# A fused attention and max-out feed-forward kernel whose whole order of work is replaced by another

## The chip, the cores and the metric

The kernel runs on one core of a Trainium2 chip. What is timed is the device time of one execution, in microseconds (us). The kernel before took 177.53 us in the median of three runs (176.96 to 178.75). TensorE does the matrix products and transposes (in a trace PE, with PEld for the loading of its weights), VectorE is DVE, ScalarE is ACT, GpSimd is POOL, and SyncE (SP) does nothing but issue DMAs from its queue.

## The reference

Four sequences of 768 tokens have eight heads of 64 features. Three of the heads (`is_retrieval`) see every earlier token, the other five see the first four tokens and the last 64. The attention's output, 3072 rows of 512, goes through a feed-forward layer that takes the larger of two products:

```
scores = scale * (q @ k.T)
mask   = full causal for retrieval heads, causal & (first 4 or last 64) for the others
a      = softmax(where(mask, scores, -1e9))
x      = (a @ v), heads side by side          # 3072 x 512
h1     = x @ w1                               # 512 x 1024
h2     = x @ w2
out    = maximum(h1, h2) @ w_out              # 1024 x 512
```

## The kernel before, in words

**Tiling.** A sequence is worked in two halves of 384 queries, so there are eight halves in all, (0,0), (1,0), (0,1), (1,1) and then both halves of sequences 2 and 3. Heads are taken in four pairs, and which heads form a pair is read from `is_retrieval` at run time. For each half the kernel loads q, k and v as f32 (`load_half`), casts them to bf16 (tiles `qb`, `vb`; lines 654 to 671), turns q and k (on PE at L680, copied back from PSUM into `qk`; later halves by DMA at L703), multiplies them into scores (L959), takes the exponential on ACT (L978, tile `at`), masks it on DVE (L997), multiplies it with v (L1022) and divides by the row sums (L1039 and L1049, tile `x`). The half's `x` is turned (L1148 or L1167, tile `xt`) and goes into the feed-forward product.

**The feed-forward product.** With max(h1, h2) = h2 + relu(h1 - h2) the kernel needs one wide product instead of two. `prep_weights` makes w12 = w1 - w2 in four column quarters (L1184, DVE alone), casts w2 to bf16 in four quarters (`w2b`, line 1191), turns these on PE (L1201, copied into `w2t`), and multiplies them with the cast output weights (`wob`, line 574) into w2o = w2 @ w_out (L1228, sixteen steps of two matmuls). From then on a half costs the "up" product with w12 (L1251, 8 blocks of 4 matmuls), the relu (L1276 on ACT, L1278 on DVE) and the "down" product, x times w2o plus the relu's output times wob (L1308). The casts and copies all go through one helper (`copy`, L382 on ACT, L384 on DVE and POOL), so in a profile they are told apart by their tiles. The very first half takes v in another way: eight casts of its rows into a spare `xt` tile, then three PE products with a shifted identity (L723) that put the rows in place, then three copies into `vb`.

**The loads at the start.** SP issues in order q, k and v of half (0,0), the two halves of w2 (1 MB each), three quarters of w_out (0.5 MB each), a half of w1, the last quarter of w_out and the other half of w1. All go through the same queue.

**What sets the order.** Nothing decides it when the kernel is built. Each step is an `Op`, registered in a fixed order and numbered. `Order.run` (line 154) walks the string `PLAN` and emits op after op: a token such as `127v` says that op 127 comes next and goes to DVE (`p` PE, `a` ACT, `v` DVE, `g` POOL, `s` SP), the digits behind a `p` name the PSUM banks, and `x0*40` says forty idle matmuls into bank 0 (`dummy`). Each engine works off its own share of that list in order, and waits at each instruction until its inputs are there; an instruction that waits holds up everything behind it on its engine. The table thus fixes three things at once: the order on each engine, which engine does a cast or copy that several could do, and which PSUM banks are used.

Of the kernel before, what the change touches and what calls it, by code (L numbers as in the profile page):

```python
# [173 lines left out]
65a x3*2 52g x3*5 8s 31a 55v x3 61g x3*2 56p3 33a 53v x4*3 4s 63a x4*2 69g x4 50p4 71a 57v x5 66p5 51a 58p6  # L174
28g x7 74p7 67a 59v x0*2 26g 76p01 75a 25g 79p23 9s 34a 37v 78a 36v 6s 35v 39a 82p45 77a 41g 85p67 84a 40a
88p10 83a 86a 13s 119v 91p54 38a 123v 89a 11s 46p6 87a 93a 42p1 47v 92a 44p7 80a 43v 16s 124p4 81a 127v 120p6
45a 131v 128p5 125a 104p2 121v 106p 94p1 90a 96p 107v 5v 95p3 10g 100p 132p7 109v 105p4 97v 101v 110p 108v
135p6 98v 149p0 111v 99v 7a 136p2 113v 134p1 103v 14s 138p 112v 133v 139p 150p 129v 137p 15s 122v 142p 151p
141p 12g 102v 140p 118v 116p4 114p7 143p 117v 115a 152p 145p 153a 147p 18s 130v 146a 212p5 144a 208p3 126v
213a 148a 221p4 209v 210p7 19s 154a 178g 192a 194g 166v 219p0 211a 156v 164v 198p6 180v 160p1 170p5 199a 220v  # L180
217p2 171a 222v 184p3 21s 165a 167g 223p7 161v 155a 157g 218a 185v 181g 172p6 162p0 195g 179a 206p5 224v 173a
193g 17s 163a 174v 186p4 200p1 176v 187a 207v 237p23 241p76 420s 201v x0 239a 244p04 214p5 190v 242a 204v 188v
245a 202v 238a 225p 247v 243a 240v 246a 249p13 20s 253p70 251a 257p26 248v 216p4 250a 252v 254a 423s 169v 168g
183a 227p 197a 196g 255a 175g 205v 177a 234p 182a 158a 256v 258a 261p31 228p 191v 259a 189v 421s 203v 263a
260v 159a 275p7 262a 270p0 235a 265p2 264v 271p 266p 229a 276p6 236s 272v 267v 281p 274v 277p 215p1 268v 24s
306a 289g 290v 305a 316g 226p 273v 295a 269v 315g 296a 424s 278v 309p3 282v 279v 231p 310a 284v 283v 23s 293p4
280v 319p5 311v 294a 313v 287p0 232v 285p2 320a 299p3 288v 356p67 286v 360p41 357a 363p05 422s 300v 339p2 358a
365a 323v 329p6 359v 22s 450g 442a 441v 337p7 364a 230s 427v 361a 333p3 434v 547s 321v 340a 433v 325p5 362a
301v 334v 449a 327p0 303v 326a 438v 454g 330v 428a 331p4 338a 328v 446a 335p2 233s 431g 448v 426a 440g 366p13
332a 447v 369p56 374p70 367a 432g 551s 307v 318a 341p4 376a 425g 668s 336v 368a 451p1 375a 439g 308v 342p 298a  # L190
291g 371a 452v 312g 343p 370a 317g 373v 800s 377p03 297g 324a 381p27 453v 385p61 378a 314g 351p5 302v 382a
292g 322a 372v 435p0 549s 383a 393p2 436v 394p 344a 304g 429p7 387a 395p 548s 384v 400p4 386a 396p 401p 437v
430a 389p01 397v 388v 406p6 669s 391a 352p 399v 398v 390a 407p7 379a 392v 353p 380v 408p 402p 354a 675s 553v
568g 412p 346p1 409v 403v 569a 413v 411v 559g 558a 405v 347p 552g 670s 579a 414v 578a 410v 556p2 404v 348p
415v 672s 557a 418p0 349a 562p3 419v 671s 416p5 563a 486p64 417v 490p72 350s 488a 493p10 443p3 495a 455p5 444v
802s 491a 457p4 494a 456v 487a 469p0 673s 458v 492a 465p7 445v 489v 470a 496p31 550s 466a 499p56 504p42 498a
507p07 500a 463p1 564v 508a 566v 502v 509a 467p5 464v 804s 501a 459p0 510v 506a 468v 461p7 503v 497a 676s 678g
460v 700a 523p1 505a 692g 462v 524p 525p 699g 691v 683a 806s 526p 511p65 561a 570g 515p23 555a 581v 519p07
345s 512a 684g 481p4 527v 696s 560v 521a 516a 571g 529v 476p6 528v 517a 580v 520a 530p7 677v 531p 518v 695s
513a 532p 582p2 522v 565a 572p1 583a 537p3 514v 682s 477p 573a 533v 586v 534v 542p 536p0 535v 688s 587g 538p  # L200
478p 543v 576v 577a 575g 539v 544v 482p 540v 807s 541v 585g 554a 545v 483p 479v 574v 546s 619p52 567v 484a
584v 623p17 626p03 697v 471p6 624a 628a 689v 704s 625a 630v 472p 627a 620a 629v 473p 355s 621a 674s 622v
631p41 652p3 633a 474v 635p70 632a 639p52 634v 636a 643p14 647p6 640a 653p 648p 803s 598p7 654v 649v 641a 656v
609p5 655v 644a 480s 645a 705v 651v 637a 590p2 650v 703s 599a 642v 588p1 591a 638v 596p3 681s 685a 680g 694v
686a 702g 679a 658p4 646v 589a 657p0 594p6 693a 475s 701a 698v 690a 659p 706v 592p7 597a 660v 595v 687s 663p
600p2 662v 593a 664v 661v 602p1 601a 799s 665v 666v 614p3 603a 926s 738p67 742p02 739a 745p41 610p 485s 743a
801s 744a 611p 746a 740a 615p 612a 741v 616p 747a 924s 748p60 617v 751p24 667s 749a 756p75 752a 759p13 775p6
761a 776p 754v 604p2 757a 762v 750a 805s 809v 825g 605p 824a 814v 835a 815g 613s 758a 606p 828s 808g 760a 753a
777p 778p 763p37 607a 755v 767p05 779v 834a 771p14 781v 782p2 819s 765a 780v 783p 768a 784p 711p7 785v 769a
787v 838s 817g 709p6 786v 811a 816g 836a 770v 821g 713p0 823a 772a 812s 837v 715p5 764a 826a 714v 707p2 841a  # L210
810g 818s 822v 820v 717p1 716a 843v 766v 708a 719p3 710a 718v 813s 773a 789p0 827v 721p5 712v 720a 831v 833a
723p2 774v 608s 839s 722v 788p6 790p 794p 733p1 791v 795v 792v 829s 796v 724p 797v 793v 725p 928s 875p47 726a
879p35 882p06 734p 881a 883a 925s 842v 840v 884a 885v 735p 876a 798s 832v 886v 877a 830v 728p2 736v 880a 878v
887p50 891p64 889a 895p73 932s 903p1 892a 890v 904p 908p0 896a 905v 729p 907v 893a 927s 906v 888a 730p 894v
897a 727s 898v 909p 899p67 913p4 901a 731v 914p1 900a 929s 854p5 910v 902v 912v 865p3 911v 930s 855v 915p 919p
848p7 916v 920v 917v 844p6 922v 931s 849a 921v 858p2 918v 845a 732s 850p0 859a 856p5 923s 955a 934v 956g 933a
852p7 940g 857v 947a 948a 846p1 938s 853a 870p4 851a 847v 939a 949g 935v 937s 871p 936a 942a 957v 958a 950v
941v 872p 954a 962v 946g 866p 873v 944s 867p 973p6 868a 943s 994p25 974v 998p70 995a 1001p14 952s 975p3 945v
996a 1003a 977p6 997v 951s 1000a 976v 965p2 1002a 971p5 999a 966v 978a 967p4 960s 972v 1004p03 968v 969p1
1006a 959s 953v 1005a 1007p72 970v 1012p65 1009a 1015p43 737s 1019p01 1008a 1011v 1031p2 874s 1017a 1032p  # L220
1010v 1033p 618s 1014a 1018v 1034p 961v 984p7 869s 1013a 1035v 1036v 1016a 1037v 1038p3 1020a 1039p 1040p
1021a 1023p56 1041v 1027p42 1042v 1025a 963p0 1022v 1029a 860p1 1043v 1028a 964v 1024a 1044p6 1030v 985p 1026v
1046p 986p 1047v 1048v 1049v 1045p2 1050p 989p3 1051v 1052v 1053v 990p 1054s 1091v 991p 1092p4 979p0 992a
1093v 993s 980p 981p 861p 982a 983s 862p 1061p5 863a 1067p6 864s 1062a 1071p2 1068a 1055p3 1081p0 1056v 1059p1
1057p5 1060v 1063p6 1058v 987a 1069p4 1064v 988s 1065p3 1070a 1076p1 1066a 1072p 1077p 1078p 1073p
"""

LAST = """
1079v 1082p 1080s 1074a 1083p 1075s 1086p5 1084v 1087p 1088p 1085s 1089a 1090a
"""  # L230


# [89 lines left out]
def tile_three_full_heads(  # L322
# [3 lines left out]
    nc = tc.nc  # L326
# [34 lines left out]
    banks = [psum.tile([128, 512], F32, name=f"ps{e}") for e in range(8)]  # L361
# [220 lines left out]
    for what in LOADS:  # L582
        kind, c = what[:2], int(what[2:]) if what[:1] == "w" else 0
# [1188 lines left out]
```

## Time and profile before

| what | value |
|---|---|
| median of three runs | 177.53 us |
| the profiled execution's own time | 178.13 us |
| its span, first to last instruction | 175.6 us |
| PE busy | 167.5 us (95%) |
| DVE busy | 117.6 us (67%) |
| ACT busy | 123.8 us (71%) |
| POOL busy | 35.4 us (20%) |
| moved by DMA | 36.14 MB, mean 206 GB/s |
| granted PE clock | 1.00 throughout |

Busy shares are means over stages that differ. Times inside the execution are counted from the first instruction; 2.53 us of the execution's time lie outside the span. A matmul's end is modelled: it is shown some 0.2 us after the next one has begun, so the start of one to the start of the next is the better measure. In the timeline a row stands for a run of like instructions, and "[0.70 <-DVE w2b L384]" means that the engine had been idle for 0.70 us until that instruction.

### The profile page before, as it was taken

To read this page: it belongs to the slowest core of one execution; us is meant where nothing else is said; L and a number is where in the kernel's file an instruction comes from. 1 tells how busy PE (TensorE), PEld (TensorE's weight loads), DVE (VectorE), ACT (ScalarE), POOL (GpSimd) and SP (SyncE) were. 2 spreads that over 40 slices of the span, in tenths; PEclk is the share of its full clock that TensorE was granted. 3 is DMA by queue.
4 is the path that set the end of the run, shared out by engine and by line. 5 is a ranking of instruction groups with operands and counts; after the bars stand their busy time and mean duration, and the time that the engine had idled before them with its cause. 6 is when DMAs were issued, how large, how long until landed. Compare 5 with 4: busy or idle time off the path is not lost.

```text
span 175.6 us, 4870 instructions
## 1 busy us (share of the span) xinstructions
PE 167.5 (95%) x1755; PEld 102.1 (58%) x1775; DVE 117.6 (67%) x327; ACT 123.8 (71%) x278; POOL 35.4 (20%) x80
## 2 busy tenths in 40 slices
PE   7899898999999999999999999999999999999993
PEld 7755644654675575667556546664665457545542
DVE  5546997876999587778978525895895377820511
ACT  3499416899899997999589789965749479214310
POOL 6850213411304803043301004200021000000000
PEclk9999999999999999999999999999999999999999
DMA  5999999999899999997299699245997236053104
GB/s 127 333 373 385 387 381 330 196 317 301 192 197 333 253 257 212 238 227 177 65 188 232 162 258 219 59 123 134 241 248 183 50 88 243 2 151 119 65 6 179
DMA packets 77661, 36.14 MB, mean 206 GB/s; under 512 B 59202, under 2 KB 72514, under 8 KB 77634
## 3 DMA queue, kind: packets, MB, share of 16 engines
q1 hardware_dynamic: 77488, 35.73, 76.7%
q8 instruction: 15, 0.25, 0.7%
q14 instruction: 12, 0.10, 0.2%
q10 hardware_dynamic: 146, 0.07, 0.1%
HBM read 25.17 MB, written 6.29 MB: 179 GB/s over the span
## 4 chain that ended last, share of the span: by engine, by line
PE 68%; DMA 11%; ACT 6%; issue 5%; POOL 4%; SPq 3%; DVE 2%; DVEq 0%; ACTq 0%; POOLq 0%
PE ps L1308 30%; PE ps L1251 21%; PE ps L959 7%; PE ps L1022 7%; DMA ld<-in_moe_w_out_dram 6%; DMA ld<-in_v_dram 4%; ACT at L978 4%; PE ps L680 2%; SPq L455 2%; POOL wob L384 2%; PE ps L1228 1%; POOL tab L612 1%; ACT ot L382 1%; ACT vb L382 1%; DMA raw<-in_is_retrieval_dram 1%
## 5 line engine op out<-in xcount | busy, mean ns | idle before, releaser
L978 ACT ACTIVATE at<-ps 128x512 bf16<-128x512 f32 (+2 forms) x134 | 64.8, 578 | 4.6 <-PE ps L959 4.1
L1251 PE MATMUL ps<-xt,w 128*128 128x384 bf16 x256 | 45.2, 326 | 0.1
L1308 PE MATMUL ps<-wob,g 128*128 128x512 bf16 (+2 forms) x192 | 43.8, 371 | 0.7 <-issue 0.3
L997 DVE TENSOR_TENSOR at<-at,tab 128x1024 bf16<-128x1024 bf16 (+5 forms) x49 | 25.1, 524 | 12.3 <-ACT at L978 11.4
L1251 PEld LDWEIGHTS <-w 128*128 128x128 bf16 x256 | 24.0, 98 | 15.9 <-issue 0.6
L1308 PEld LDWEIGHTS <-g 128*128 128x128 bf16 x200 | 18.3, 98 | 19.6 <-issue 0.2
L1278 DVE TENSOR_SCALAR g<-ps 128x384 bf16<-128x384 f32 x34 | 18.5, 553 | 13.5 <-PE ps L1251 13.0
L382 ACT COPY ot<-ps 128x512 f32<-128x512 f32 (+1 forms) x16 | 9.0, 571 | 22.5 <-PE ps L1308 19.1
L1308 PE MATMUL ps<-w2o,xt 128*128 128x512 bf16 (+2 forms) x90 | 24.0, 370 | 0.5
L384 POOL CAST qb<-ld 128x384 bf16 (+1 forms) x31 | 13.6, 472 | 53.3 <-DMA ld<-in_k_dram 28.4
L1049 DVE TENSOR_TENSOR x<-ps,rez 128x192 f32 x64 | 22.7, 354 | 2.0 <-DVE rez L1039 0.5
L1022 PEld LDWEIGHTS <-at 128*128 128x128 bf16 x477 | 17.9, 97 | 4.7 <-DVE at L997 0.3
L1022 PE MATMUL ps<-vb,at 128*128 128x65 bf16 x387 | 19.3, 194 | 0.0
L1276 ACT ACTIVATE g<-ps 128x384 bf16<-128x384 f32 x30 | 14.5, 495 | 6.6 <-PE ps L1251 6.4
L959 PE MATMUL ps<-qk 64*128 64x128 bf16 (+1 forms) x330 | 19.1, 229 | 0.0
L959 PEld LDWEIGHTS <-qk 64*128 64x128 bf16 x330 | 12.1, 94 | 9.2 <-issue 7.0
L382 ACT CAST qb<-ld 128x384 bf16 (+1 forms) x32 | 12.8, 458 | 2.1 <-DMA ld<-in_q_dram 1.7
L1308 PEld LDWEIGHTS <-xt 128*128 128x128 bf16 x100 | 8.8, 98 | 8.1
L382 ACT COPY qk<-ps 128x384 bf16<-128x384 bf16 (+1 forms) x17 | 10.2, 631 | 2.3 <-PE ps L680 1.9
L384 DVE COPY ot<-ps 128x512 f32<-128x512 f32 (+1 forms) x9 | 6.0, 672 | 7.3 <-PE ps L1308 6.4
L680 PE MATMUL ps<-tab,qb 128*128 128x128 bf16 x120 | 10.0, 219 | 0.7 <-POOL qb L384 0.4
L384 POOL CAST vb<-ld 128x192 bf16 x15 | 6.1, 421 | 20.3 <-issue 10.2
(76 smaller groups left out, 162.7 us busy)
## 6 DMA issues: line engine op xcount, KB each, us to landing
ld<-in_v_dram SPq DMA_DIRECT2D x21, 256.0 KB, 5.4
ld<-in_moe_w_dram SPq DMA_DIRECT2D x4, 1024.0 KB, 12.2
out_dram<-ot SPq DMA_DIRECT2D x16, 256.0 KB, 3.6
ld<-in_q_dram SPq DMA_DIRECT2D x5, 768.0 KB, 8.1
ld<-in_k_dram SPq DMA_DIRECT2D x5, 768.0 KB, 6.9
ld<-in_q_dram SPq DMA_DIRECT2D x9, 256.0 KB, 4.5
ld<-in_k_dram SPq DMA_DIRECT2D x9, 256.0 KB, 4.4
ld<-in_moe_w_out_dram SPq DMA_DIRECT2D x4, 512.0 KB, 11.0
```

Of the source, the lines that this page charges most:

```text
L382: nc.scalar.copy(out=out, in_=in_)
L384: eng[e].tensor_copy(out=out, in_=in_)
L680: nc.tensor.transpose(to[:, i], qbs[:, T["qb", n, hf] % NQB, t, i].rearrange("p h d -> p (h d)"), ident)
L959: nc.tensor.matmul(to.rearrange("p (i c) -> p i c", c=128), lhsT=lhsT, rhs=q_of(n, i, m)[rows], start=bk not in under, stop=True, skip_gro ...
L978: nc.scalar.activation(out=at[:, bk, 0:w], in_=bank(("ps", b, hf, t), part=bk)[:, 0:w], func=ACT.Exp, scale=scale,)
L997: eng[e].tensor_tensor(out=at, in0=at, in1=tbl, op=ALU.mult)
L1022: nc.tensor.matmul(po[:, hh, i - NT * hf, :], lhsT=ats[:, T["at", b, hf, t] % NAT, bk, e * 128:(e + 1) * 128], rhs=rhs, start=first, stop= ...
L1049: nc.vector.tensor_tensor(out=xs[:, HALVES.index((b, hf)) % NX, :, bass.ds(heads[2 * p + hh], 1), :], in0=po[:, hh, :, 0:D].unsqueeze(2), ...
L1251: nc.tensor.matmul(bank(key)[:, 0:HALF], lhsT=w[:, kc, fc * 128:(fc + 1) * 128], rhs=xts[:, HALVES.index((b, hf)) % NXT, :, kc, :], start= ...
L1276: nc.scalar.activation(out=g, in_=ph, func=ACT.Relu)
L1278: nc.vector.tensor_scalar_max(out=g, in0=ph, scalar1=0.0)
L1308: nc.tensor.matmul(bank(key)[:, cols], lhsT=lhsT, rhs=(w2o if kind == "x" else wob)[:, c, cols], start=(e == 0), stop=(e == len(steps) - 1),)
```

## The change

`PLAN` is another list. It has the same 1081 ops, so the same loads, casts, products and stores, in another order and with other PSUM banks; 147 of them, casts and copies above all, go to another engine than before. The idle matmuls go from 81 to 75. `dummy` gets a second parameter that would make one idle matmul several times as wide; every call leaves it at 1, so that an idle matmul is what it was. Lines move by one to four.

```
-0s x0*3 1s x0*5 2s x0*40 3s 30a 32v 68g x0*3 70a 54v x0 48p0 62a 27g x1 72p1 49v x2*4 29g 60a 73v x2 64p2 x3*2
+0s x0*3 1s x0*5 3s x0*36 2s 52a 30v x0*3 68a 54v x0 70g x0 32a x0 56p0 62a 26v 25g x1 48p1 57a 72p2 x3 49v
...
-    def dummy(e):
-        nc.tensor.matmul(banks[e][:, 0:128], lhsT=warm, rhs=warm, start=True, stop=True)
+    def dummy(e, m=1):
+        nc.tensor.matmul(
+            banks[e][:, 0:128 * m].rearrange("p (m c) -> p m c", m=m), lhsT=warm,
+            rhs=warm.unsqueeze(1).to_broadcast([128, m, 128]), start=True, stop=True,
+        )
```

**First place: the loads on SP at the start.** Before:

```order
L442 DMA ld<-in_q_dram 128x8x192
L442 DMA ld<-in_k_dram 128x8x192
L442 DMA ld<-in_v_dram 128x8x192
L547 DMA ld<-in_moe_w_dram 128x4x512 x2
L568 DMA ld<-in_moe_w_out_dram 128x2x512 x3
```

And now:

```order
L446 DMA ld<-in_q_dram 128x8x192
L446 DMA ld<-in_k_dram 128x8x192
L551 DMA ld<-in_moe_w_dram 128x4x512
L446 DMA ld<-in_v_dram 128x8x192
L551 DMA ld<-in_moe_w_dram 128x4x512
L572 DMA ld<-in_moe_w_out_dram 128x2x512 x3
```

The first half of w2 goes ahead of v. The second half of w2 keeps its place, and so does everything behind it up to the order of the three w_out quarters among themselves and of the two w1 halves (columns 512 to 1023 of w1 now come first).

**Second place: DVE where w12 is made.** `w_144` is the quarter of w1 - w2, `x` the divided output of the first half, `xt` its turned copy, `g` a relu, `w2o` the copy of a finished column block of w2 @ w_out. Before:

```order
L384 COPY w2t<-ps_167 128x1024
L384 COPY w2t<-ps_165 128x1024
L1184 TENSOR_TENSOR w_144<-ld 128x4x256
L1049 ISA
L1049 TENSOR_TENSOR x<-ps_163,rez 128x3x64
L1184 TENSOR_TENSOR w_144<-ld 128x4x256
L384 COPY xt<-ps_164 128x512
L1184 TENSOR_TENSOR w_144<-ld 128x4x256 x2
L1278 TENSOR_SCALAR g<-ps_163 128x384
```

And now:

```order
L1053 TENSOR_TENSOR x<-ps_167,rez 128x3x64
L1188 TENSOR_TENSOR w_144<-ld 128x4x256
L388 COPY xt<-ps_161 128x512
L388 CAST wob<-ld 128x1024
L1188 TENSOR_TENSOR w_144<-ld 128x4x256
L1282 TENSOR_SCALAR g<-ps_164 128x384
L388 CAST w2o<-ps_165 128x512
L388 CAST w2o<-ps_163 128x512
L1188 TENSOR_TENSOR w_144<-ld 128x4x256 x2
```

The last cast of w_out (`wob`), which was POOL's, is now on DVE, and two copies of w2o, which were ACT's, stand ahead of the last two quarters of w12. On PE the first up block now comes ahead of the last four of the sixteen w2 @ w_out steps (before, all sixteen came first), and six of the eight up blocks ahead of the first turns of the next half (before, five).

Further up on DVE, where the third and the fourth quarter of w2 were cast one right after the other, a copy of v into `vb` now stands between the two casts; the casts of the first and second w_out quarter are both on DVE (the second was ACT's); the copies of the third and fourth turned quarter have gone from DVE to ACT. Of v's eight casts POOL has three (before one), ACT one (before four).

**Third place: SP in the middle of half (1,0).** Loads and stores share the queue. Each v row is a third of one half's v (128 of its 384 tokens). Before:

```order
L1336 DMA out_dram<-ot 128x512
L455 DMA ld<-in_v_dram 128x8x64 x3
L442 DMA ld<-in_k_dram 128x8x192
L455 DMA ld<-in_v_dram 128x8x64
L1336 DMA out_dram<-ot 128x512
L442 DMA ld<-in_q_dram 128x8x192
```

And now:

```order
L1340 DMA out_dram<-ot 128x512
L459 DMA ld<-in_v_dram 128x8x64 x3
L446 DMA ld<-in_k_dram 128x8x192
L1340 DMA out_dram<-ot 128x512
L459 DMA ld<-in_v_dram 128x8x64 x2
L446 DMA ld<-in_q_dram 128x8x192
```

The single v row behind the k load was the last third of v for half (0,1), op 22. It now stands behind another store, and the three v rows further up are no longer ops 24, 424 and 23 but 421, 548 and 424: op 548 is a third of v for half (2,0), which came much later before.

Behind these places every later stage is ordered anew as well, up to the scores of half (3,0); from there on the kinds of work and their engines are the same in both lists, with neighbours exchanged here and there.

More of the change, by code (lines that the diff above doesn't have):

```diff
@@ L178 @@
[L178 to L182, printed above, removed]
@@ new lines @@
+51a x6*2 74p6 28g 59v 66p7 x0 76p01 27g 67a 75v 79p23 77a 6s 123v 119a 9s 82p45 124p7 83a 120p6 80a 125v 85p04
+84a 121v 16s 34g 41a 38g 88p27 81a 35v 40g 36v 78a 91p56 39v 87a 37v 89a 11s 44p3 92a 13s 127v 93a 42p1 45v
+86a 128p4 131v 43a 46p2 129a 5v 132p5 47v 134p6 90a 7v 149p3 133a 105p0 110p 95p1 111v 100p 94p4 112v 96p
+136p2 101v 113v 139p 103v 14s 10g 97v 137p 102v 104p7 99v 106p 98v 150p 107v 151p 109v 140p 108v 135p5 15s
+126v 114p0 116p1 115a 138p 117v 141p 12v 142p 130v 217p4 145p 152p 218v 221p7 146v 17s 219p1 153v 222a 118v
@@ new lines @@
+576v 554a 477p 535v 513a 522v 682s 516a 478p 534v 512a 518v 561a 619p54 695s 571a 514v 623p63 479a 626p10
+537p2 689v 621a 542p 536p7 543v 587g 625a 538p 582p4 806s 697v 620a 585g 481p3 539v 545v 577a 583a 541v 482p
+676s 575g 544v 540v 628a 586v 483p 624a 584v 627a 630v 546s 622v 560a 631p52 635p47 484v 565a 639p06 647p1
+637a 629v 648p 471p3 640a 649v 703s 650v 632a 567a 651v 472p 633a 641a 634v 704s 652p7 636a 642v 473p 638v
+485s 643p05 658p1 474v 644a 653p 657p2 645a 801s 654v 600p6 646v 656v 659p 681s 592p4 655v 601a 660v 596p0
@@ new lines @@
+1004p43 969p2 968v 1006a 959s 953v 1005a 1007p15 970v 1012p60 1009a 1015p73 737s 1019p42 1008a 1011v 1031p5
+874s 1017a 1032p 1010v 1033p 618s 1014a 1018v 1034p 961v 984p1 869s 1013a 1035v 1036v 1016a 1037v 1038p3 1020a
+1039p 1040p 1021a 1023p06 1041v 1027p75 1042v 1025a 963p4 1022v 1029a 860p2 1043v 1028a 964v 1024a 1044p6
+1030v 985p 1026v 1046p 986p 1047v 1048v 1049v 1045p5 1050p 989p3 1051v 1052v 1053v 990p 1054s 1091v 991p
+1092p7 979p4 992a 1093v 993s 980p 981p 861p 982a 983s 862p 1061p0 863a 1067p6 864s 1062a 1071p5 1068a 1055p3
@@ L226 @@
+1081p4 1056v 1059p2 1057p0 1060v 1063p6 1058v 987a 1069p7 1064v 988s 1065p3 1070a 1076p2 1066a 1072p 1077p
+1078p 1073p
 """
 LAST = """
-1079v 1082p 1080s 1074a 1083p 1075s 1086p5 1084v 1087p 1088p 1085s 1089a 1090a
+1079v 1082p 1080s 1074a 1083p 1075s 1086p0 1084v 1087p 1088p 1085s 1089a 1090a
 """
```

83 lines of the change are left out of this document (36 added, 47 removed).

## Prediction

> **What bounds the kernel now.** I read first the page's busy times, then busy time by stretch, cut at events that the timeline shows: the first scores, the first step of w2 @ w_out, the first up block, the scores of half (1,0), of half (0,1), and so on to PE's last matmul. Behind the time stand PE, DVE and ACT.
>
> ```profile
> PE 167.5 (95%) x1755; PEld 102.1 (58%) x1775; DVE 117.6 (67%) x327; ACT 123.8 (71%) x278; POOL 35.4 (20%) x80
> ```
>
> ```profile
> core 0: us, PE busy (x) PEld busy (x) DVE busy (x) ACT busy (x) POOL busy (x), PEclk, DMA share, GB/s
> 10.37:20.71 10.34, 9.48 (x145) 6.02 (x146) 6.61 (x17) 8.57 (x19) 1.36 (x4) 1.00 1.05 388
> 20.71:29.81 9.10, 8.04 (x51) 3.96 (x49) 7.63 (x15) 2.88 (x4) 2.82 (x2) 1.00 1.07 363
> 29.81:36.28 6.47, 6.47 (x57) 4.36 (x55) 5.53 (x14) 5.54 (x16) 2.15 (x7) 1.00 1.02 245
> 36.28:49.63 13.35, 13.14 (x160) 8.07 (x161) 10.96 (x36) 12.49 (x30) 3.00 (x6) 1.00 1.02 251
> 49.63:62.83 13.20, 13.06 (x141) 7.99 (x141) 10.53 (x27) 12.91 (x31) 6.33 (x14) 1.00 1.00 259
> 62.83:117.76 54.93, 54.45 (x651) 33.75 (x656) 40.54 (x114) 48.40 (x108) 9.99 (x21) 1.00 0.81 185
> 117.76:172.63 54.87, 54.26 (x465) 30.20 (x469) 30.02 (x83) 27.60 (x60) 1.66 (x4) 1.00 0.51 136
> ```
>
> Length less PE busy is PE's idle time: 0.86, 1.06, 0, 0.21, 0.14, 0.48 and 0.61 us, 3.36 in 162.26 us. The work on PE is the same in both lists, so whatever the new order does well, it can win about these 3.4 us and no more (a little more hides in rows that run slower than their neighbours); what it does badly has no such limit. 1.92 of the 3.36 lie before 29.81 us, while the loads arrive. There DMA is full (shares of 1.05 and 1.07), and the timeline tells what PE waits for:
>
> ```profile
> 16.61 1.06 PE L1201 MATMUL ps<-tab,w2b 128*128 128x128 bf16 x16
> 18.36 0.62 PE L1201 MATMUL ps<-tab,w2b 128*128 128x128 bf16 x8 [0.70 <-DVE w2b L384]
> 18.82 1.27 PE L1022 MATMUL ps<-vb,at 128*128 128x65 bf16 x36
> 19.93 0.61 PE L1201 MATMUL ps<-tab,w2b 128*128 128x128 bf16 x8
> 20.37 0.53 PE L1022 MATMUL ps<-vb,at 128*128 128x65 bf16 x12
> 20.75 5.64 PE L1228 MATMUL ps<-wob,w2t 128*128 128x512 bf16 x23
> 26.23 0.83 PE L1148 MATMUL ps<-tab,x 128*128 128x128 bf16 x12
> 27.92 1.89 PE L1228 MATMUL ps<-wob,w2t 128*128 128x512 bf16 x8 [0.86 <-POOL wob L384]
> 29.65 3.41 PE L1251 MATMUL ps<-xt,w 128*128 128x384 bf16 x20
> 34.05 0.33 PE L680 MATMUL ps<-tab,qb 128*128 128x128 bf16 x3
> 36.28 0.51 PE L959 MATMUL ps<-qk 64*128 64x128 bf16 x12
> ```
>
> Two waits stand out: 0.70 us for the third quarter of w2, 0.86 us for the last cast of w_out on POOL.
>
> **The change, part by part.**
>
> *The loads.* The engines that cast a load start when it lands:
>
> ```profile
> 8.28 1.11 ACT L382 CAST qb<-ld 128x192 bf16 x4 [0.37 <-DMA ld<-in_k_dram]
> 10.68 0.88 DVE L384 CAST xt<-ld 128x192 bf16 x3 [0.31 <-DMA ld<-in_v_dram]
> 13.39 1.30 DVE L384 CAST w2b<-ld 128x1024 bf16<-128x1024 f32 x2 [1.83 <-DMA ld<-in_moe_w_dram]
> 15.52 1.34 DVE L384 CAST vb<-ps 128x512 bf16<-128x512 f32 x2 [0.83 <-PE ps L723]
> 17.61 1.29 DVE L384 CAST w2b<-ld 128x1024 bf16<-128x1024 f32 x2 [0.76 <-DMA ld<-in_moe_w_dram]
> ```
>
> k has landed at 8.28, v 2.40 us later, the first half of w2 2.71 later, the second half, of the same size, 4.22 later: 1.51 longer than its twin. In the two microseconds from 13 to 15 us one packet of instructions went through the DMA engines, and everything behind that moment is late:
>
> ```profile
> q8 instruction: 1, 0.02, 3.4%
> ```
>
> With the first half of w2 ahead of v I get 8.28 + 2.71 = 10.99 for it and 13.39 for v. The second half has the same bytes ahead of it as before and stays at 17.61. If the packet now falls on v, v lands at up to 14.90.
>
> *PE up to the second half of w2.* Before, scores, the placing of v (L723) and the first 16 turns of w2 were through at 16.61 + 1.06 = 17.67. Now the turns come between the third and the fourth score tile and one block of three placing matmuls (3 x 0.216 = 0.65) is put behind the third quarter, so PE is through at 17.0 if nothing waits. The third quarter can be cast from 17.61 to 18.26 (half of 1.30), so PE stands for 1.2 us, where it stood for 0.70. Then comes the block of 0.65, and the fourth quarter, whose cast now has a copy of v ahead of it (0.61 + 0.64 + 0.65 behind 17.61, that is 19.5), is turned from 19.6 to 20.05. PE has by then done no weighted product (L1022), of which 36 matmuls were done before: this part is behind by about 0.8 us.
>
> *PE up to the first up block.* What remains ahead of the first up block are 12 of the 16 steps (24 x 0.216 = 5.2), all 48 weighted matmuls (1.27 + 0.53 less two tails of 0.2 = 1.4) and the 12 turns of x (0.66): from 20.05 to 27.3. DVE has to have its third quarter of w12 ready by then:
>
> ```profile
> 19.58 0.65 DVE L384 CAST wob<-ld 128x1024 bf16<-128x1024 f32 x1
> 21.61 1.53 DVE L1049 TENSOR_TENSOR x<-ps,rez 128x192 f32 x4 [0.21 <-DVE rez L1039]
> 24.35 1.23 DVE L1184 TENSOR_TENSOR w<-ld 128x1024 bf16<-128x1024 f32 x1
> 28.42 2.36 DVE L1184 TENSOR_TENSOR w<-ld 128x1024 bf16<-128x1024 f32 x2 [1.11 <-DMA ld<-in_moe_w_dram]
> 27.10 1.01 ACT L382 COPY xt<-ps 128x1024 bf16<-128x1024 bf16 x1 [4.37 <-PE ps L1148]
> ```
>
> The first w1 half lands at 24.35, as before. From 21.7 (its casts of w_out and the first weighted products done) DVE has eight divisions at 0.38 and four reciprocals, to about 25.3, then 1.14 for the quarter: 26.4, 0.9 us in hand. The 0.86 us that PE stood for POOL's cast are gone, because the cast is on DVE and has four up blocks and one more quarter beside it; what is late next is ACT's copy of the turned x (1.01 us behind turns that end at 26.1), at 27.1, still in time.
>
> *PE up to the scores of half (1,0).* Four steps (1.73) and six up blocks (24 matmuls, 0.65 a block as 3.41 less its tail over 5) end at 32.9, nine turns at 33.4; before, the same set ended at 34.05. The up blocks 0 and 1 need the quarters that DVE makes last, behind a relu and the two copies of w2o that it has been given: 26.4 + 0.4 + 0.6 + 1.14 + 0.47 + 1.2 + 1.14 = 31.4, against a need at 31.6. That is thin. Then k of half (1,0) sets a floor:
>
> ```profile
> 25.74 2.13 POOL L384 CAST wob<-ld 128x1024 bf16<-128x1024 f32 x1 [4.34 <-DMA ld<-in_moe_w_out_dram]
> 31.05 0.64 POOL L384 CAST qb<-ld 128x192 bf16 x2 [3.18 <-DMA ld<-in_q_dram]
> 33.31 1.51 POOL L384 CAST qb<-ld 128x192 bf16 x5 [1.63 <-DMA ld<-in_k_dram]
> ```
>
> It lands at 33.31 whatever PE does, the casts take 1.5 us and the turn with its copy 1.0: scores not before 35.8. I take 35.9, so **-0.4 us** against 36.28. The ends: 0 if DVE's thin place slips, -0.5 at the floor.
>
> POOL's 2.13 us are the odd one of twins, as the same cast shows five microseconds earlier:
>
> ```profile
> 20.35 1.04 POOL L384 CAST wob<-ld 128x1024 bf16<-128x1024 f32 x1 [8.98 <-DMA ld<-in_moe_w_out_dram]
> ```
>
> The difference, 1.09, is about one quarter of w12 on DVE (1.14 from start to start), and two of these were worked beside it. The Trainium skill (SBUF — State Buffer, "Who interferes with whom") says why: a DVE instruction with two SBUF inputs and a GpSimd instruction that reads SBUF take turns on one port, and whichever comes second waits until the first is done. By that rule the change has a price that I have not counted: its last two quarters of w12 (30.3 to 32.5) now run while POOL casts q (31.05), which they did not before; each quarter could stand 0.3 us for a cast of POOL's, and the sum would be +0.2 rather than -0.4. The trace agrees on the lock; on this meeting no run here shows it. I give it 2 chances in 10 within the forecast's case; at 177.7 it lies inside that case's range and moves none of the chances below.
>
> *Everything behind 36.28 us.* Idle time there is 1.44 us. The order is new up to the scores of half (3,0), about 118 us, and I have no row for what it will be; below, the ends are 0 idle (-1.4) and the first rival below (+2.0). I take the row's own 1.44: no difference. The six idle matmuls left out stand before 10 us, where PE waits for k: nothing.
>
> The sum, against the profiled execution: 178.13 - 0.4 = 177.7. That execution lies 0.6 above the median of 177.53, so in the median **177.1 us**.
>
> **The rivals.**
>
> *Slower: v of half (0,1) comes late.* The chain of waits goes through this load; the row at 62.33 is where it is back on PE.
>
> ```profile
> 49.47 6.69 DMA ld<-in_v_dram
> ...
> 62.33 0.50 PE ps L680 x6
> ```
>
> That third of v now has a third of v for half (2,0) and one more store ahead of it, 0.52 MB, at 255 GB/s (the two stretches from 36.28) 2.05 us. It lands at 58.2 instead of 56.16. If DVE, ACT and POOL need the time from there to 62.33 as they did, all of it reaches PE: 177.1 + 2.05 = 179.2. For it speaks the chain, and ACT's 12.91 of 13.20 us: it can't catch up. Against it: 6.2 us for eight casts of about 0.3 is much, most of that chain is a full ACT, and the new order may put those casts later on purpose. It decides from the point where the casts of v end after about 61 us.
>
> *Faster: the idle time of the start goes.* If PE's 1.92 us before 29.81 and a third of the later 1.44 went: 177.53 - 2.4 = 175.1. For it: the idle time is there. Against it: the second half of w2 at 17.61 and k at 33.31 are set by DMA, which has no idle time to give.
>
> *The delay falls elsewhere.* Twelve PE instructions fewer move the moment of the fetch. If it misses these loads, all behind come 1.5 us earlier, k at 31.8, and PE's floor with it: 175.6. Against it: by 13 us PE has done about the same number of instructions in either order.
>
> **How the numbers follow.** A measurement of this kernel tells about 1% (1.8 us) from no change. The forecast has 0.57 (with 1.4 to either side, 175.7 to 178.5), the late v 0.24, the start's idle time 0.12, the delay elsewhere 0.07. The range, 175.4 to 179.5, leaves out most of the start's idle time and the part of the late v that goes beyond its price. Faster by over 1% (below 175.75): the last two cases and a little of the forecast, 0.2. Slower by over 1% (above 179.3): half of the late v and a tail of the forecast, since a second new stage may slip as well, 0.2. Within 1%: 0.6.
>
> **What would show it.** Right: DVE's first cast of w2 near 11.0 and its third at 17.6; PE idle for 1.2 us before the third quarter's turns; no wait for the last cast of w_out; scores of half (1,0) near 35.9; idle time behind that near 1.4. Wrong: the second half of w2 near 16.1, up blocks that wait for w12 between 31 and 33 us, or PE idle near 60 us for v.

## The result and the profile after

The changed kernel takes **176.71 us** in the median of 15 runs (176.39 to 177.45), the kernel before in the same comparison 177.76 (176.96 to 178.75): a ratio of 0.9948, 95% interval [0.9929, 0.9967]. Medians here are over all executions of a kernel; the ratios leave out the few that took over 1.5% longer than its quickest. The profiled execution took 176.59 us with a span of 174.8; before it was 178.13 with 175.6. The page of the changed kernel, first its span, then the busy times:

```profile
span 174.8 us, 4844 instructions
PE 166.9 (95%) x1747; PEld 101.3 (58%) x1769; DVE 120.4 (69%) x333; ACT 122.6 (70%) x277; POOL 31.6 (18%) x75
```

The first thing to see is in the two pairs of numbers. The time fell by 1.54 us from one profiled execution to the other, the span by 0.8 only. What is left of the time beside the span was 2.53 us and is 1.79. The prediction never looked at that part.

**The start, which the prediction spoke of.** When the loads land, by the first casts of each (timeline of DVE, then of POOL, changed kernel):

```profile
11.01 0.69 DVE L388 CAST w2b<-ld 128x1024 bf16<-128x1024 f32 x1 [0.33 <-DMA ld<-in_moe_w_dram]
17.24 0.69 DVE L388 CAST w2b<-ld 128x1024 bf16<-128x1024 f32 x1 [2.11 <-DMA ld<-in_moe_w_dram]
13.43 0.93 POOL L388 CAST xt<-ld 128x192 bf16 x3 [2.86 <-DMA ld<-in_v_dram]
```

The first half of w2 is there at 11.0 and v at 13.4; the second half comes at 17.2, 3.8 us behind v, where its twin took 2.7. PE, at the turns of the third quarter of w2, at the first up block, and at the first scores of half (1,0):

```profile
17.99 0.62 PE L1205 MATMUL ps<-tab,w2b 128*128 128x128 bf16 x8 [0.96 <-ACT vb L386]
27.13 0.81 PE L1255 MATMUL ps<-xt,w 128*128 128x384 bf16 x4
35.77 0.51 PE L963 MATMUL ps<-qk 64*128 64x128 bf16 x12
```

PE stands 0.96 us for the third quarter (the releaser named, ACT's copy of v, is the wait ahead of it), and no longer for the last cast of w_out: there is no bracket at 27.13. Where w12 is made, DVE and then POOL:

```profile
26.97 1.22 DVE L1188 TENSOR_TENSOR w<-ld 128x1024 bf16<-128x1024 f32 x1
28.58 1.28 DVE L388 CAST w2o<-ps 128x512 bf16<-128x512 f32 x2
29.77 2.50 DVE L1188 TENSOR_TENSOR w<-ld 128x1024 bf16<-128x1024 f32 x2
30.59 1.89 POOL L388 CAST qb<-ld 128x192 bf16 x2 [8.23 <-DMA ld<-in_q_dram]
33.04 0.64 POOL L388 CAST qb<-ld 128x192 bf16 x2 [0.56 <-DMA ld<-in_k_dram]
```

Two of POOL's casts take 1.89 us beside the last two quarters of w12 and 0.64 without company.

**By stage**, cut at the starts of the scores of halves (0,0), (1,0), (0,1) and (1,1): the changed kernel, then the kernel before (its middle row, 36.28 to 49.63, stands in the prediction).

```profile
9.95:35.77 25.82, 24.47 (x248) 14.33 (x249) 21.36 (x45) 17.11 (x37) 5.13 (x9) 1.00 1.06 342
35.77:48.74 12.97, 12.86 (x157) 7.92 (x161) 11.08 (x36) 12.27 (x30) 3.22 (x7) 1.00 1.10 273
48.74:69.91 21.17, 21.01 (x250) 13.54 (x252) 18.17 (x51) 19.04 (x43) 6.31 (x15) 1.00 1.06 260
```

```profile
9.95:36.28 26.33, 24.41 (x249) 14.44 (x249) 20.18 (x44) 17.41 (x39) 6.74 (x12) 1.00 1.05 344
49.63:70.82 21.19, 20.99 (x246) 12.98 (x247) 16.81 (x45) 19.77 (x44) 7.77 (x17) 1.00 1.04 256
```

25.82 against 26.33, 12.97 against 13.35, 21.17 against 21.19: 0.5 us up to the scores of half (1,0), 0.4 in the stage behind them, nothing after that. From these two traces I formed the theory of two gains, both of the order, that make up the whole. The experiments left the second standing, and little of the first.

### The profile page after: what moved, and what is told of

It reads as the page before. It is cut to its first block, busy times and chain, and to the rows that moved or that the text cites. A ratio compares the mean times of both kernels' runs of the same rounds, so it can differ in the third digit from the quotient of the medians.

```text
span 174.8 us, 4844 instructions
## 1 busy us (share of the span) xinstructions
PE 166.9 (95%) x1747; PEld 101.3 (58%) x1769; DVE 120.4 (69%) x333; ACT 122.6 (70%) x277; POOL 31.6 (18%) x75
## 4 chain that ended last, share of the span: by engine, by line
PE 80%; ACT 10%; DMA 4%; issue 2%; DVE 1%; SPq 0%; ACTq 0%; DVEq 0%
PE ps L1312 31%; PE ps L1255 24%; PE ps L963 7%; PE ps L1026 7%; ACT at L982 7%; PE ps L1232 4%; DMA ld<-in_k_dram 4%; PE ps L684 3%; PE ps L1152 1%; ACT vb L386 1%; DVE at L1001 1%; PE ps L1205 1%; ACT qk L386 0%; ACT w2b L386 0%; ACT vx L386 0%
## 5 line engine op out<-in xcount | busy, mean ns | idle before, releaser
L982 ACT ACTIVATE at<-ps 128x512 bf16<-128x512 f32 (+2 forms) x134 | 64.7, 578 | 7.8 <-PE ps L963 7.7
L1255 PE MATMUL ps<-xt,w 128*128 128x384 bf16 x256 | 45.7, 326 | 0.0
L1312 PE MATMUL ps<-wob,g 128*128 128x512 bf16 (+2 forms) x192 | 44.5, 370 | 0.5 <-issue 0.2
L1001 DVE TENSOR_TENSOR at<-at,tab 128x1024 bf16<-128x1024 bf16 (+5 forms) x49 | 24.2, 507 | 6.8 <-ACT at L982 6.5
L1282 DVE TENSOR_SCALAR g<-ps 128x384 bf16<-128x384 f32 x32 | 17.4, 552 | 15.7 <-PE ps L1255 15.4
L1280 ACT ACTIVATE g<-ps 128x384 bf16<-128x384 f32 x32 | 15.4, 497 | 12.5 <-PE ps L1255 12.3
L386 ACT COPY ot<-ps 128x512 f32<-128x512 f32 (+1 forms) x15 | 8.7, 580 | 17.2 <-PE ps L1312 16.1
L386 ACT CAST qb<-ld 128x192 bf16 (+1 forms) x35 | 12.8, 433 | 2.4 <-DMA ld<-in_q_dram 1.7
L388 DVE COPY ot<-ps 128x512 f32<-128x512 f32 (+1 forms) x10 | 6.7, 673 | 9.6 <-PE ps L1312 8.8
L388 DVE COPY qk<-ps 128x384 bf16<-128x384 bf16 (+1 forms) x14 | 9.8, 724 | 1.9 <-PE ps L684 1.9
L684 PE MATMUL ps<-tab,qb 128*128 128x128 bf16 x120 | 8.8, 219 | 1.0 <-DVE qb L388 0.8
L388 POOL CAST vb<-ld 128x192 bf16 x13 | 4.4, 361 | 29.0 <-DMA ld<-in_v_dram 28.3
```

The source lines that it names most:

```text
L386: nc.scalar.copy(out=out, in_=in_)
L388: eng[e].tensor_copy(out=out, in_=in_)
L684: nc.tensor.transpose(to[:, i], qbs[:, T["qb", n, hf] % NQB, t, i].rearrange("p h d -> p (h d)"), ident)
L982: nc.scalar.activation(out=at[:, bk, 0:w], in_=bank(("ps", b, hf, t), part=bk)[:, 0:w], func=ACT.Exp, scale=scale,)
L1001: eng[e].tensor_tensor(out=at, in0=at, in1=tbl, op=ALU.mult)
L1255: nc.tensor.matmul(bank(key)[:, 0:HALF], lhsT=w[:, kc, fc * 128:(fc + 1) * 128], rhs=xts[:, HALVES.index((b, hf)) % NXT, :, kc, :], start= ...
```

## The experiments

Each kernel was compared with the kernel before on the same chip. "Outside" is the median, over a kernel's executions, of the time less the span. The kernel before stands in it with 2.44 to 2.48 us, by comparison, and the changed kernel with 1.79.

**The two parts of the order, one at a time.** The tables were joined at the first scores of half (1,0); of the ops only three copies of that half lie on different sides of the joint in the two tables. Banks were renamed behind it.

```
 head_new:  0s x0*3 1s x0*5 3s x0*36 2s ...   (new)  | 237p.. ... (old)
 head_old:  0s x0*3 1s x0*5 2s x0*40 3s ...   (old)  | 237p.. ... (new)
```

> The new list up to the scores of half (1,0), the old list from there. Theory (two gains, an early one of 0.5 us from the last cast of w_out on DVE and the up blocks pulled ahead, and a later one of 0.4 us in the stage behind the scores): these scores start at 35.8 us as in the changed kernel, the rest takes as long as in the kernel before, and the time is 0.5 us under it (177.2). Rival (the new start alone is the whole change): 0.9 us under it (176.8). Rival (what is won early is lost at the next load): as before.

> The old list up to the scores of half (1,0), the new list from there. Theory of two gains: scores at 36.3 us as before, then 0.4 us won up to the scores of half (0,1), so 177.4 us. Rival (the new start is the whole change): as before. Rival (the early 0.5 us are not needed, since a load sets the scores of half (0,1)): these scores at 48.7 us all the same and 176.8 us.

Measured: with the new start and the old rest 177.24 us, ratio 0.9969 [0.9951, 0.9988]; with the old start and the new rest 176.93, ratio 0.9953 [0.9935, 0.9971]. The stage behind the joint in both profiles, the new start first, and PE at the joint of the second:

```profile
35.92:49.46 13.54, 13.54 (x161) 8.13 (x162) 11.42 (x38) 12.60 (x31) 2.82 (x6) 1.00 1.10 269
```

```profile
36.22:49.19 12.97, 12.97 (x160) 7.92 (x160) 9.89 (x32) 12.12 (x29) 3.44 (x7) 1.00 1.09 263
36.22 0.51 PE L962 MATMUL ps<-qk 64*128 64x128 bf16 x12 [0.39 <-ACT qk L385]
```

The second gain is there and goes with the new rest: 12.97 against 13.54 here, 12.97 against 13.35 in the two kernels whole. But as a time both kernels come out elsewhere than that. The one with the new start and the old rest sits exactly on my number, for a wrong reason: its median span is 175.5 us, longer than the 175.1 of the kernel before in the same comparison. The other has 175.2, of which 0.39 are the joint's own. What both have won lies outside the span: 1.75 and 1.74 us against 2.48.

Little of the second gain is idle time. PE is busy for the whole of both stretches, 13.54 and 12.97 us, with the same work but for one idle matmul; the 24 turns of q and k in it, for example, take 1.8 us with the old rest and 1.5 with the new.

**The two loads.** First half of w2 and v exchanged in the old list alone, and exchanged back in the new one.

```
 loads_only (old list):  -2s x0*40 3s   +3s x0*40 2s
 loads_back (new list):  -3s x0*36 2s   +2s x0*36 3s
```

> The kernel before with its list, only the first half of w2 issued ahead of v. Theory (the swap pays only together with the order on the engines): the first half of w2 at 11.0 us is of no use, v lands at 13.4 and PE, which in the old list places v before it turns w2, stands for about 1.5 us (0.5 to 2.5): 178.3 to 180. Rival (the swap is where the gain is): scores of half (1,0) at 35.8 us and 177.2 us.

> The changed kernel, only v issued ahead of the first half of w2 again. Theory: the turns of the first two quarters of w2, which the new list puts ahead of the fourth score tile, wait until 14.5 us instead of 12; PE loses 1 to 2 us there, and 0.7 of it comes back since PE stands less for the second half of w2: 177.2 to 178.2 us, 0.5 to 1.5 over the changed kernel. Rival (DMA sets everything up to 18 us, the order of these two does not matter): within 0.2 of the changed kernel.

Measured: 180.32 us, ratio 1.0140 [1.0103, 1.0178], and 178.51 us, ratio 1.0019 [0.9993, 1.0044], which is 1.8 us over the changed kernel. ACT and PE of the first, then PE of the second:

```profile
13.43 0.35 ACT L382 CAST xt<-ld 128x192 bf16 x1 [2.84 <-DMA ld<-in_v_dram]
14.32 0.38 PE L928 MATMUL ps<-tab 128*128 128x512 bf16 x1 [1.31 <-ACT at L978]
```

```profile
14.04 1.89 PE L1205 MATMUL ps<-tab,w2b 128*128 128x128 bf16 x16 [2.00 <-DVE w2b L388]
```

In the old list ACT has a cast of v ahead of its exponentials, stands 2.84 us for the late v, and the scores behind it have no bank to go to. In the new list with the loads exchanged back PE stands 2.00 us for w2. Load order and engine order belong together.

The waits are not the whole price. In both profiles the granted PE clock, 1.00 throughout in all the other profiles, fell for a while; the line of the clock in 40 slices, from the page of loads_back, then of loads_only:

```profile
PEclk9996999999999999999999999999999999999999
PEclk9998799999999999999999999999999999999999
```

In the first it stands at 0.50 for 3.4 us from 13.8 us on, in the second for as long from 16.8. Not every execution had that. Five of the twelve of loads_back kept a mean clock of 1.00 and took 177.20 to 177.43 us, 0.5 to 0.7 over the changed kernel and at the low end of what was expected; the other seven show 0.99 and took 178.48 to 180.25. Of the six of loads_only one kept 1.00 and took 178.89, the others, at 0.99, 180.07 to 181.93. So with the clock held the exchange costs about 0.6 us in the new list, and 1.3 in the old one by that single execution; the fall of the clock costs over a microsecond more. In the first PE was standing at that moment (the 2.00 us above), in the second its 1.31 us had ended 2.4 us before; whether that brings the clock down was not tested. No other execution with its clock on record shows less than 0.995.

**The form of the idle matmul.** Up to here every kernel with the small outside time was also written with the new form of `dummy`, and every one with the large outside time with the old. The two forms build the same instructions; they were exchanged on both lists.

```
 new_idle (old list):  -def dummy(e):  +def dummy(e, m=1):
 old_idle (new list):  -def dummy(e, m=1):  +def dummy(e):
```

> The kernel before with the new form of the idle matmul and the old list; every instruction is the same as before. Of the four runs so far the three with the new form spend 1.75 us of their time outside the span, the kernel before and the one run with the old form 2.4 to 2.5. Theory (most of the 0.9 us lies outside the span and hangs on something that goes with the new file, not on the order): 1.75 us outside, a span of 175.05 as before, 176.9 us. Rival (it hangs on the order): 2.5 us outside and 177.6 us.

> The changed kernel with the old form of the idle matmul, its instructions unchanged. Theory: span of 174.9 us as in the changed kernel and 2.5 us outside it, so 177.4 us. Rival (it hangs on the order): 1.8 us outside, 176.7 us.

Measured: 177.72 us with 2.44 outside, ratio 1.0002 [0.9968, 1.0035], and 176.78 us with 1.78 outside, ratio 0.9962 [0.9940, 0.9984]. My theory fell; it goes with the list. But the two kernels are also second profiles of the old and of the new program, and the second profile of the old one shows something else. Its stages:

```profile
9.74:35.22 25.48, 24.47 (x250) 14.35 (x250) 20.72 (x44) 17.40 (x39) 5.68 (x12) 1.00 1.05 344
35.22:48.58 13.36, 13.15 (x161) 8.07 (x162) 11.17 (x36) 12.46 (x30) 2.85 (x6) 1.00 1.05 269
48.58:70.42 21.84, 20.99 (x247) 12.99 (x247) 16.88 (x45) 19.89 (x44) 7.81 (x17) 1.00 1.02 254
```

The first stage takes 25.48 us here and 26.33 in the profile of before, with the same instructions. The reason, on POOL, DVE and PE of this run:

```profile
25.46 1.04 POOL L387 CAST wob<-ld 128x1024 bf16<-128x1024 f32 x1 [4.33 <-DMA ld<-in_moe_w_out_dram]
25.50 2.08 DVE L1187 TENSOR_TENSOR w<-ld 128x1024 bf16<-128x1024 f32 x1
26.64 1.89 PE L1231 MATMUL ps<-wob,w2t 128*128 128x512 bf16 x8
68.11 0.51 PE L683 MATMUL ps<-tab,qb 128*128 128x128 bf16 x6 [0.64 <-POOL qb L387]
```

In the profile of before POOL's last cast of w_out stood at 25.74 with 2.13 us, PE stood 0.86 us for it, and DVE's quarter, from the timeline of that profile, took its usual 1.2:

```profile
25.76 1.22 DVE L1184 TENSOR_TENSOR w<-ld 128x1024 bf16<-128x1024 f32 x1
```

Here POOL is first by 0.04 us and takes 1.04, DVE's quarter takes 2.08, and PE does not wait at all: DVE has time there, POOL's cast has none. In the profile of before POOL's row starts 0.02 us ahead as well, and yet it is POOL that waits: so close together, the starts of the rows do not tell which of the two will. The wait that the prediction made most of is a race that some executions win. (Two more profiles of kernels with this part of the old list, pad_dve and head_old, lost it, with DVE 0.07 and 0.18 us ahead and 0.87 and 0.90 us of PE's time.) What was won is not kept in this execution: with the scores of half (1,0) a microsecond earlier than before, PE stands 0.64 us at 68 for k of half (1,1), and the scores of half (1,1) start at 70.42 where before they started at 70.82. That load landed anywhere from 64.7 to 66.8 in the profiles of the old list with v issued first; why, no run here tells.

**The last cast of w_out, moved two ways.** Back to POOL in the new list, and to ACT in the old one, where ACT is idle.

```
 cast_back (new list):  -12v   +12g
 act_cast (old list):   -12g   +12a
```

> The changed kernel with the last cast of w_out on POOL again, as before. Theory: the first up block does not wait for it any more in the new list, the steps that do are pulled behind it; POOL's cast takes 1.0 to 2.1 us from 25.4 us, so the last four steps of w2 @ w_out can start at 27.5 at the latest while PE needs them at about 27.5: the loss is 0 to 0.3 us. Rival (this cast's move is where the early half microsecond comes from): PE stands 0.8 us near 27 us and the time is 0.5 to 0.8 us over the changed kernel.

> The kernel before, only the last cast of w_out moved from POOL to ACT, which is idle for 4.4 us there. Theory (a meeting decided by chance: POOL's cast and a quarter of w12 on DVE start within 0.04 us of each other; in the profile of before POOL came second, took 2.13 us and PE stood 0.86 us, in the profile of the run with the new form of the idle matmul, instruction for instruction the same kernel, DVE came second, took 2.08 us for two quarters in a row without a gap, and PE did not stand): without the meeting no execution loses the 0.86 us, the scores of half (1,0) start at 35.2 to 35.5 us and the spread of the spans (174.4 to 177.0) becomes narrower; but k of half (1,1) lands at 66.4 us or later all the same, so the median span goes down by 0.3 us at most and the time is 177.2 to 177.6. Rival (the wait removed is what the changed kernel won): 0.9 us under before. Rival (ACT pays for the cast): slower.

Measured: 176.65 us, ratio 0.9957 [0.9938, 0.9976], the same as the changed kernel; and 177.14 us, ratio 0.9979 [0.9951, 1.0006]. In the new list the cast on POOL meets a w12 quarter as well (POOL, then DVE):

```profile
25.57 1.59 POOL L388 CAST wob<-ld 128x1024 bf16<-128x1024 f32 x1 [3.00 <-DMA ld<-in_moe_w_out_dram]
26.58 1.66 DVE L1188 TENSOR_TENSOR w<-ld 128x1024 bf16<-128x1024 f32 x1
```

but the steps that need it stand behind an up block, so that nobody waits. What the new list does better here is the place of the up block, not the engine of the cast. In the old list with the cast on ACT nothing meets (DVE, then ACT):

```profile
25.44 1.22 DVE L1184 TENSOR_TENSOR w<-ld 128x1024 bf16<-128x1024 f32 x1
25.46 1.04 ACT L382 CAST wob<-ld 128x1024 bf16<-128x1024 f32 x1 [3.07 <-DMA ld<-in_moe_w_out_dram]
```

the scores of half (1,0) start at 35.18, and the median span is 174.6 us against 175.1 before; the interval of the ratio still holds 1. The outside time is 2.46 as before. The spread did not become clearly narrower (174.3 to 175.9 against 174.5 to 176.4).

**The fetch of instructions.** In the new list every row of idle matmuls was made of a quarter as many, rounded up, four times as wide: 32 in place of 75. That is 43 fewer, not the 45 of the expectation.

```
-for _ in range(int(times or 1)):
-    self.dummy(int(spot))
+left = int(times or 1)
+while left > 0:
+    self.dummy(int(spot), min(4, left))
+    left -= 4
```

> The changed kernel with every row of idle matmuls made of a quarter as many, four times as wide: 45 matmuls and 45 loads of weights fewer for PE in the same time. Theory (the second half of w2 is late because a fetch of PE's instructions at 13.5 us goes through the full DMA engines): the fetch comes at about 16.5 us, the second half of w2 lands near 16.1 instead of 17.2, PE's wait of 0.96 us for it goes to under 0.3; but the scores of half (1,0) are set by k, which has the late fetch ahead of it still, and start at 35.6 to 35.8: within 0.3 us of the changed kernel. Rival (what PE waits for there is on the path to the end): 0.7 to 1 us under the changed kernel. Rival (the fetch has nothing to do with it): the half lands at 17.2.

Measured: 176.97 us, ratio 0.9971 [0.9939, 1.0002], no gain over the changed kernel. The profiled execution is one of its quickest, with a span of 174.5 us where they go from 174.5 to 177.2. The DMA queues between 15 and 17 us, then DVE and PE:

```profile
q8 instruction: 1, 0.02, 3.4%
15.97 0.69 DVE L390 CAST w2b<-ld 128x1024 bf16<-128x1024 f32 x1 [0.97 <-DMA ld<-in_moe_w_dram]
19.46 1.04 PE L1234 MATMUL ps<-wob,w2t 128*128 128x512 bf16 x4 [0.92 <-DVE wob L390]
35.44 0.51 PE L965 MATMUL ps<-qk 64*128 64x128 bf16 x12
```

With fewer PE instructions the packet went through two microseconds later, and the second half of w2 landed at 15.95 instead of 17.21, 2.7 us behind v like its twin. So the delay does belong to that fetch. PE's wait of 0.96 us for w2 is gone, and a new one of 0.92 has come for the first cast of w_out, whose load landed at 18.68 (18.56 in the changed kernel): the delay moved on to the next load. The Trainium skill (Runtime: NRT & Kernel Launch, "Instruction fetch mechanics") calls the cost of crossing from one block of instructions to the next mostly hidden. PE itself does not stand for the block here, which agrees; but in a full DMA queue the load behind it is 1.1 to 1.5 us late.

**The parts put together.** The old start with its cast on ACT, and the new rest.

```
 mixed (old start, new rest):  -12g   +12a
```

> The old list up to the scores of half (1,0) with the last cast of w_out on ACT, the new list from there. Theory: the old start without its meeting reaches these scores 0.3 us earlier than the new one, counted from the first scores (25.5 against 25.8 us), and the new list behind them has no load that takes it back: span 174.5 to 174.7, 1.75 us outside it, 176.3 to 176.5 us. Rival (the new list from there waits for its own loads, timed to the later start): 176.7 to 176.9, as the kernel with the old start and the new rest.

Measured: 176.68 us, ratio 0.9953 [0.9932, 0.9973], 1.71 outside and a median span of 174.9: the changed kernel's time. It does not decide between the two, since the joint has a price of its own:

```profile
36.01 0.51 PE L962 MATMUL ps<-qk 64*128 64x128 bf16 x12 [0.58 <-DVE g L1281]
```

These scores wait 0.58 us at the joint, and k of half (1,1) landed at 65.93 in this execution (64.70 in the changed kernel's), the longest of the nine with a span of 175.8. Whether a list planned as a whole with the old start would be better stays open.

**What lies outside the span.** The list decides over it, yet either half of the new list is enough. What differs in all these programs is how many instructions the compiled program has for each engine: moving casts changes the counts by a few, those of the instructions that only wait for a semaphore among them. The counts are those of the compiled files; a trace holds only what was executed.

| kernel | DVE | ACT | POOL | SP | outside, us |
|---|---|---|---|---|---|
| before, new_idle, loads_only, act_cast | 4158 | 573 | 422 | 205 | 2.44 to 2.46 |
| the changed one, old_idle, few_idle, cast_back, loads_back | 4165 | 565 | 417 | 197, 198 | 1.73 to 1.79 |
| head_new | 4162 | 578 | 417 | 204 | 1.75 |
| head_old, mixed | 4160 | 562 | 421 | 198 | 1.74, 1.71 |
| pad_dve | 4160 | 573 | 422 | 205 | 2.06 |
| both_pads | 4160 | 577 | 422 | 205 | 1.76 |

PE is not in the table: few_idle, which executes 86 PE instructions fewer than the changed kernel, is in the same row with it. The last two rows are the test. To the kernel before two tiny instructions on DVE were added; then, on top of the kernel with the cast on ACT, these two and four tiny ones on ACT.

```
+for _ in range(3):
     nc.vector.memset(ones, 1.0)
 ...
 nc.scalar.activation(out=warm, in_=warm, func=ACT.Exp)
+for _ in range(4):
+    nc.scalar.copy(out=warm, in_=warm)
```

> The kernel before with two more tiny instructions on DVE ahead of all work (a one-column constant is written three times). The programs with 2.44 us outside their span have 4158 instructions for DVE, all others 4160 or more, with 1.75; on POOL it is 422 against 421 or fewer, on SP 205 against 204 or fewer. Theory (what lies outside the span hangs on how long DVE's program is): 4160 instructions, 1.75 us outside, 176.9 us. Rival (it is POOL's or SP's length, or the order itself): 2.44 us outside, 177.6 us.

> The old list with the last cast of w_out on ACT, the two more tiny instructions on DVE, and four more tiny ones on ACT (a one-column copy onto itself, at 4 us, where ACT waits for q). DVE's two took 0.4 of the 0.7 us. Counted in blocks of 64 instructions, DVE's program ended 62 into a block before and ends at 0 into the next with them; ACT's ended 61 into one and ends 1 into the next now; all programs with 1.75 us outside end ACT's 50 to 53 or 2 into a block. Theory (the rest of what lies outside hangs on ACT's length in the same way): 1.75 us outside, and with a span of 174.6 a time of 176.3 to 176.4, under the changed kernel with none of its order. Rival (the rest is POOL's or SP's, 422 and 205 as before): 2.05 us outside, 176.7. Rival (DVE's 0.4 was no matter of the length): 2.45 outside, 177.1.

Measured: with DVE's two, 2.06 us outside (12 executions, 2.02 to 2.18, against 2.37 to 2.56 for the kernel before), which is between what the theory and the rival said, and 177.25 us, ratio 0.9982 [0.9952, 1.0012]. With ACT's four as well, 1.76 (1.69 to 1.83) and **176.66 us**, ratio 0.9942 [0.9911, 0.9972]. That is the changed kernel's time, with the old list, one cast moved and six instructions that do nothing; its median span, 174.85, is that of the kernel before in the same comparison (174.8). So DVE's two instructions are worth 0.38 us and ACT's four, which were not run alone, 0.30 on top; together they are as much as the 0.65 us by which the changed kernel is better outside its span. That these instructions do it is shown, and since they run at 4 to 5 us, while both engines wait for q, it is hardly their work but their number, or that they move what stands behind them; why this matters is not shown. It is not a matter of longer or shorter: 562 and 565 instructions for ACT go with the small outside time as well as 577 and 578. The counts 4158 and 573 lie 2 and 3 below a multiple of 64 and all others in these two columns at or above one, or well below. That is a pattern in the counts and no more; the packets of instructions in the traces are of 8 and 16 KB. A fetch of instructions at the end of the program is one candidate that no run tested. The Trainium skill (the same page and section) says that a jump to a place outside the blocks on hand waits for a fetch; the rows of a trace end with the span, and none shows it.

## Why the prediction was right, and where it was not

The forecast was 177.1 us and no change that can be told; it came out as 176.71, and since the interval of the ratio leaves out 1, this half percent could be told. Its events at the start were nearly all right, its account of the gain was not.

- *The loads.* 10.99 for the first half of w2, 13.39 for v: 11.0 and 13.4 measured. The second half was put at 17.61 and landed at 17.21: the fetch cost it 1.1 us more than its twin, not 1.5. The fetch as the cause, a guess from one packet then, is borne out by the run with fewer idle matmuls.
- *PE up to the first up block.* A wait of 1.2 us for the third quarter: 0.96 (the load came 0.4 us earlier). The fourth quarter's turns at 19.6: 19.19. First up block at 27.3: 27.13, and it waited for nothing.
- *PE up to the scores of half (1,0).* The thin place on DVE held: the last two quarters ran from 29.77 to 32.3 against a forecast of 30.3 to 32.5. Scores at 35.9: 35.77.
- *The port rule.* The meeting of POOL's casts of q with the last quarters of w12 took place, but POOL was the one that waited (1.89 us for 0.64), DVE's pair took 2.50 where it had taken 2.36, and nothing was late for it. The price of up to 0.6 us that the prediction left uncounted was 0.1 on DVE and none on PE. That "whichever comes second waits" can go either way from one execution to the next I read in the rule and did not apply to the wait of 0.86 us on which I built.
- ***-0.4 us against 36.28.*** Right against that trace, and the wrong yardstick. 36.28 belongs to an execution that lost the race at 25.7 us. One that won it started these scores at 35.22, earlier than the changed kernel. The removed wait is a removed risk.
- *Everything behind 36.28: no difference.* There was one, 0.4 us in the stage from the scores of half (1,0) to those of half (0,1), with the new rest only. I had taken that stage's idle time over because I had no row for it; most of the 0.4 us was in PE's busy time, which I had put down as "a little". With the start counted in as it falls, won race or lost, the median spans come within 0.2 us of each other where both lists ran together (175.0 in old_idle and 174.95 in cast_back, 175.1 before).
- *The sum.* It was made in the span, and the rest of the time was carried over as it was. **That is the mis-sized term**: 0 for what lies outside the span, measured -0.65, of a whole of -0.8 against the 177.53 that the forecast starts from and -1.05 against the 177.76 of the same comparison. The profile before gave 2.53 us for it; nothing there could have told that it would change, and I did not ask. That the number came out near is in part luck: of the -0.4 in the span, built in the main on the wait that turned out a race, the medians show 0.1 (175.0 against 175.1) to 0.4 (1.05 less 0.65), and the larger part of the gain was in no term.
- *The rivals.* The late v: that third of v was in use from 56.8 us on rather than 58.2 (POOL's row below), no row of PE between 50 and 72 us of the changed kernel shows a wait, so the 2.05 us never came. The error was to add its bytes to the old landing time: the k load ahead of it was issued at 46.9 instead of 48.5, and there was room in the queue. The start's idle time did not go: 0.96 us stood where 0.70 had been, as DMA had it. The fetch did not fall elsewhere: it went through at 13.5 us, with six idle matmuls fewer; it took a change of 43 to move it.

```profile
56.76 1.36 POOL L388 CAST vb<-ld 128x192 bf16 x4 [1.86 <-DMA ld<-in_v_dram]
```

## What to carry to other kernels

Where a change is worth less than a microsecond, take the time apart into the span and what lies outside it before explaining it by anything in the trace; here six to eight tenths of the gain lay where the trace has no rows. A wait seen in one profiled execution may be one side of a race: look for two engines that start within a tenth of a microsecond on work that holds the same thing, and take a second profile of the same program before its removal is counted as a gain. And in a stage that is full of loads, work that is pulled forward can be given back at the next load, as at 68 us in one profile here. When a kernel gets slower, look at the granted clock before the whole price is put down to a wait.

## What the runs showed of the hardware that was not expected

- Six instructions that do nothing, two on DVE and four on ACT, made the time outside the span 0.68 us shorter (2.44, 2.06, 1.76). Programs that differ by a few such instructions can differ by 0.4% in time with the same median span.
- One 16 KB packet of instructions in a full DMA queue made a 1 MB load 1.1 to 1.5 us late; moved by two microseconds, it made PE wait for the next load instead (0.96 us for w2, then 0.92 for w_out).
- The same program, with POOL and DVE starting 0.02 to 0.04 us apart, gave the delay of a microsecond once to POOL (2.13 us for 1.04) and once to DVE (2.08 for 1.2), and only one of these reaches PE.
- With v and the first half of w2 exchanged in either list, 12 of 18 executions had a mean granted PE clock of 0.99 and took over a microsecond longer than those of the same kernel that kept 1.00; in the two that were profiled the clock stood at 0.50 for 3.4 us. What brought it down is open.
